# Block 0's MLP down in seven products at the end, the last mixer between its upward groups, second products accumulated on copies in PSUM

## The chip, the cores and the metric

The kernel runs on one core of a Trainium2 chip. The metric is the device time of one execution in microseconds (us); the median of three runs is 498.36 us (498.01 to 498.67). A core has five engines with their own in-order instruction streams: TensorE (PE, matmuls), VectorE (DVE), ScalarE (ACT), GpSimd (POOL) and SyncE (SP, which here only issues transfers). PSUM has eight banks into which matmuls write; SBUF holds everything else on chip.

## What is computed

The reference, cut to what matters; all numbers are float32, with 2048 rows (S), 512 columns (D), 32 heads of 16 and a hidden width of 1376 (F):

```
xn  = layernorm(x)
q, k, v = heads of xn @ wqkv
phi(t)  = where(t > 0, t + 1, exp(t)) + 1e-6
kv  = einsum("bhsd,bhse->bhde", phi(k), v);  z = sum over s of phi(k)
s   = (phi(q) @ kv) / (phi(q) . z + 1e-6), heads joined, @ wo
h   = gelu(layernorm(xn) @ w1)          # the mixer
hs  = h with its four column groups shifted by +1, -1, +2, -2 rows, @ w2
x1  = xn + hs
h2  = gelu(layernorm(x1) @ w3) @ w4     # the MLP: "up" by w3, "down" by w4
out = x + s * silu(x1 + h2)
```

## The kernel before

**Rows and precision.** The 2048 rows are four blocks of 512, each of four row tiles of 128 (QT = 4, NQ = 4). A float32 product is made of three matmuls: each operand is split into a rounded high part and the remainder (`rounded`: ScalarE copies the high part, VectorE subtracts it), and `products` issues high x high, high x low and low x high into one PSUM bank. TH = 256 is half a block.

**Seven products.** Most large products are cut in 2 x 2 and made of seven products of half size in place of eight; the sums and differences of the quarters are formed beforehand. The function `seven` runs one such group in three banks: pb, pe and pa. The first product, a11·b11, stands in pb and is copied to SBUF (p1) by ScalarE; a12·b21 goes to pa, and VectorE adds pa and p1 to the first result. The rest of pb and pe follows with more products accumulated on the same bank, each after a copy of what stood there. The mixer (`mix2`), the ways up (`up_pair`, `up_late`) and the attention (`attend_pair`) use it; the projections have their own version.

**The plan.** The kernel function does not issue instructions in the order in which it names them. Each call adds an operation to a list with an estimated duration. `Plan.emit` then walks the list with a model of the engines: TensorE's operations follow roughly their named order (within a window), the other engines' operations get due times worked back from it, and each may open its buffers only some microseconds ahead of its due time. The table SOONER shifts the due times of single operations, by their number in the list. Buffers come from pools with slots: 90 of 512 columns in SBUF ("p"), 6 of 256 ("h"), and in PSUM two pools of four banks, "mm" and "acc".

**The order of the work.** First the keys, queries and their gram matrices for all blocks; then the mixer of blocks 0 to 3 (`join_a`, `mix1`, `forms`, `mix2`), with the folding of kv and wo into one matrix M between them; then the MLP and the attention together. In the MLP the hidden width is eleven slices of 128, the last with 96: five pairs (s, s + 5), NS = 5, and a last one. `turn_y` prepares a block's normalised rows, `load_pair` the slices of w3, `up_last` and five ways up follow.

Block 0 differs from the others (LATE = 1, 2, 3). Its ways up (`up_pair`) put gelu's result out twice, as high part and as full value, and VectorE forms the remainder. Its way down (`down`) follows slice by slice between the ways up: for each slice and each of four row tiles three matmuls of 512 columns, accumulated over all eleven slices in the four banks of the "acc" pool (tiles acc0_0 to acc0_3). Its w4 slices are read through `load_w4` (six of them split early, `make_w4`, and stored in the memory array w4d; five made on the way).

Blocks 1 to 3 go up with `up_late`, which keeps gelu's results in SBUF, and are taken down at the end in the order LINE = (2, 3, 1): `down_forms` builds the sums of the quarters and their high and low parts, `down_late` makes the seven products, with banks from both PSUM pools. Block 1 (SPILL) is written to the array hd by `put` and read back at the end; its sums s1 and s3 are made by an accumulating transfer on POOL's queue (`gather`). Its attention result goes through the array sod in the same way.

The attention runs in pairs of row tiles at places given by ATT (`turn_q`, `forms_q`, `attend_pair`). `gate` multiplies by the attention result, adds x by a transfer and stores the output; for block 0 it uses tanh and two VectorE operations, for the late blocks silu and one.

Of the kernel before, what the change touches and what calls it, by code (L numbers as in the profile page):

```python
# [8 lines left out]
F32 = mybir.dt.float32  # L9
# [5 lines left out]
P = 128  # L15
# [9 lines left out]
class Tile:  # L25


    def __init__(self, plan, tag, name, dtype, width, rows=P):
        self.plan, self.tag, self.name, self.dtype, self.width, self.rows = plan, tag, name, dtype, width, rows
        self.ap = None  # L30
        self.log = []
        self.left = 0
        self.end = 0.0
        self.psum = tag in plan.psum
        self.early = plan.early

# [49 lines left out]
class Plan:  # L86
# [198 lines left out]
    def emit(self, first, lead, reserve, window, ahead, table=()):  # L285
# [16 lines left out]
        table = 0  # L302
        done = set()
        slip = 0.0
        left = len(ops)
        while left:
# [56 lines left out]
            for t in op.tiles:  # L363
                if t.ap is None:
                    tag = t.tag
                    if tag in slots:
                        t.slot = slots[tag].pop(0)[1]
                        tag += str(t.slot)
                    t.ap = self.pools[t.tag].tile([t.rows, t.width], t.dtype, tag=tag, name=t.name)
# [42 lines left out]
def linear_attn_gated_by_mixer(  # L412
# [62 lines left out]
    def bank(name):  # L475
        return pl.new("mm", name, F32, 512)[:, :]
# [154 lines left out]
    def spread(b):  # L631
# [7 lines left out]
        ps = pl.new("mm", f"ab{b}", F32, 512)[:2 * QT, :P]  # L639
# [289 lines left out]
    def seven(name, z, prod):  # L929

        pa, pb, pe = (bank(f"{n}{name}").cols(0, TH) for n in ("pa", "pb", "pe"))
        p1, p5, u2 = (pl.new("h", f"{n}{name}", F32, TH).all for n in ("p1", "p5", "u2"))

        def go(ps, x, y, start=True):
            products(ps, prod(x, y), start, more=not start)

# [212 lines left out]
    def make_w4(f):  # L1149
        n = rows(f)  # L1150
        st, (hi, lo) = piece(f"w4_{f}_s").rows(n), rounds(f"w4_{f}")
        pl.load(st, w4[f * P:f * P + n, :])
        rounded(hi.rows(n), lo.rows(n), st)
        for k, v in enumerate((hi, lo)):
            keep_in(w4d[f], k, v.rows(n), n)
        return hi.rows(n), lo.rows(n)

    def load_w4(b, f):
        n = rows(f)
        if b == 0 and f not in early_f:  # L1160
            W4[b, f] = make_w4(f)
            return
        W4[b, f] = tuple(v.rows(n) for v in rounds(f"w4_{b}_{f}"))
        for k, v in enumerate(W4[b, f]):
            pl.fetch(v.f32, w4d[f][:n, k * 512:(k + 1) * 512])
# [104 lines left out]
    def up_last(b):  # L1270
# [4 lines left out]
        late = b in LATE  # L1275
        if late:
            HL[b] = ge.rows(n)
        else:
            hi, lo = rounds(f"f{b}_{f}")
        for t in range(2):  # L1280
            h = t * TH, (t + 1) * TH
            ps = bank(f"a{b}_{f}_{t}").cols(0, TH).rows(n)
            ks = y[f"b1{t + 1}"] + y[f"b2{t + 1}"]
            products(ps, [AF3["last"][c] + ks[c] for c in range(NC)])
            if not late:
                pl.act(hi.cols(*h).rows(n), ps, AF.Gelu_apprx_tanh)
            pl.act(ge.cols(*h).rows(n), ps, AF.Gelu_apprx_tanh)
        if late:
            if b in SPILL:
                put(b, 10, HL[b], n)  # L1290
            return
        split(lo.rows(n), ge.rows(n), hi.rows(n))
        H3[b, f] = (hi, lo, n)

    def up_pair(b, s):
        hi, lo = zip(*(rounds(f"f{b}_{f}") for f in (s, s + NS)))
        full = [piece(f"gf{b}_{f}") for f in (s, s + NS)]
        c1, c2 = full
        z = c1.cols(0, TH), c1.cols(TH, 512), c2.cols(TH, 512)
        ps = seven(f"{b}_{s}", z, lambda x, y: [AF3[s][x][c] + YT[b][y][c] for c in range(2)])  # L1300
        pl.act(hi[0], c1, AF.Gelu_apprx_tanh)
        pl.act(c1, c1, AF.Gelu_apprx_tanh)
        split(lo[0], c1, hi[0])
        pl.act(hi[1].cols(TH, 512), z[2], AF.Gelu_apprx_tanh)
        pl.act(z[2], z[2], AF.Gelu_apprx_tanh)
        pl.act(hi[1].cols(0, TH), ps, AF.Gelu_apprx_tanh)
# [629 lines left out]
```

## Time and profile before

| | |
|---|---|
| median of three runs | 498.36 us |
| span of the profiled execution | 496.4 us |
| instructions in it | 9885 |
| TensorE busy | 490.6 us (99%) |
| VectorE busy | 438.4 us (88%) |
| ScalarE busy | 373.4 us (75%) |
| GpSimd busy | 123.6 us (25%) |
| transfers | 117.44 MB, 237 GB/s on average |

The time of the profiled execution outside its span is not recorded; the median of the runs is 1.96 us above that span. Names in the profile are those of the program's tiles with their numbers left out: acc are block 0's accumulators, pb, pe and pa the banks of the ways up, pbm of the mixer, pbs, pes and pas of the attention, pbd, ped and pad of the late ways down. Most operations are recorded in helpers, so their line is that of the helper (L146 for a matmul, L168 for ScalarE, L191 and L201 for VectorE, L225 for POOL's transfers); the tile tells them apart. A matmul's duration in the profile includes its way through the array, so the pitch is read from start to start.

### The profile page before, as it was taken

How to read it: one execution, taken by the hardware profiler on the slowest of the kernel's cores; microseconds unless marked ns; L12 is line 12 of the kernel's file. 1: busy time of each engine (PE TensorE's matmuls, PEld its weight loads, DVE VectorE, ACT ScalarE, POOL GpSimd, SP SyncE). 2: the span in 40 equal slices, each digit the busy share in tenths (PEclk: the TensorE clock that was granted, in tenths of full speed). 3: DMA queues.
4: the chain of work that ended last, by engine and by line, in shares of the span. 5: the costliest groups of instructions: out<-in, count | busy, mean ns of one | idle time of the engine just before them, and what ended most of it. 6: DMA issues, size and time to landing. Idle time of an engine off the chain costs nothing.

```text
span 496.4 us, 9885 instructions
## 1 busy us (share of the span) xinstructions
PE 490.6 (99%) x3244; PEld 447.0 (90%) x3244; DVE 438.4 (88%) x874; ACT 373.4 (75%) x845; POOL 123.6 (25%) x214
## 2 busy tenths in 40 slices
PE   8999999999999999999999999999999999999996
PEld 6778888888888999899889999999999999999996
DVE  5998997889989669999999999999999899796864
ACT  5999999677887599999988567765686877565531
POOL 1384404276930232133200021100000000143420
PEclk9999999999999999999999999999999999999999
DMA  7869696999974999999988499984634699599996
GB/s 229 303 187 297 133 296 183 237 287 269 329 220 100 236 310 248 273 252 290 337 268 247 158 194 298 247 262 138 183 114 147 215 336 332 114 226 283 278 224 182
DMA packets 87082, 117.44 MB, mean 237 GB/s; under 512 B 10328, under 2 KB 39160, under 8 KB 87032
## 3 DMA queue, kind: packets, MB, share of 16 engines
q1 hardware_dynamic: 75512, 96.11, 59.6%
q0 software_dynamic: 11520, 20.71, 24.9%
q8 instruction: 25, 0.41, 0.4%
q14 instruction: 25, 0.20, 0.1%
HBM read 72.66 MB, written 39.93 MB: 227 GB/s over the span
## 4 chain that ended last, share of the span: by engine, by line
PE 97%; DMA 1%; SPq 1%; ACT 0%; DVE 0%; issue 0%; ACTq 0%
PE pb L146 12%; PE pbd L146 9%; PE h L146 9%; PE g L146 9%; PE acc L146 6%; PE pe L146 6%; PE pbx L146 6%; PE ped L146 5%; PE pbm L146 5%; PE pbs L146 5%; PE q L146 3%; PE pa L146 3%; PE pex L146 3%; PE k L146 3%; PE pad L146 3%; PE pes L146 2%
## 5 line engine op out<-in xcount | busy, mean ns | idle before, releaser
L225 POOL DMA_DIRECT2D xo<-x1d x12 | 10.9, 950 | 166.2 <-DVE xo L191 118.5
L225 POOL DMA_DIRECT2D th<-in_x x14 | 12.2, 895 | 45.0 <-DVE th L201 23.1
L225 POOL DMA_DIRECT2D o<-xnd x16 | 14.0, 887 | 37.5 <-DVE o L191 13.5
L168 ACT ACTIVATE th<-xo 128x512 f32<-128x512 f32 (+1 forms) x16 | 9.7, 614 | 15.9 <-DVE xo L201 10.1
L225 POOL DMA_DIRECT2D zacc<-ke x12 | 12.9, 1073 | 31.4 <-DMA zacc<-ke 10.4
L191 DVE TENSOR_TENSOR ht<-h,abc 128x512 f32<-128x512 f32 x16 | 11.0, 690 | 7.5 <-PE h L146 7.4
L225 POOL DMA_DIRECT2D xt<-nrow x16 | 14.6, 1288 | 8.4 <-ACT k12h L168 4.1
L196 POOL TENSOR_SCALAR w<-mv 128x4 f32<-128x4 f32 (+2 forms) x10 | 2.5, 254 | 40.7 <-ACT sq L168 40.4
L168 ACT ACTIVATE y<-o,nm,rs 128x512 f32<-128x512 f32 x16 | 12.4, 814 | 0.2 <-POOL nm L196 0.2
L168 ACT ACTIVATE p<-pb 128x256 f32<-128x256 f32 x20 | 7.6, 381 | 5.8 <-PE pb L146 5.4
L168 ACT ACTIVATE ht<-ht 128x512 f32<-128x512 f32 x16 | 10.0, 626 | 2.1 <-DVE ht L191 2.0
L168 ACT ACTIVATE sq<-o,mv 128x512 f32<-128x512 f32 x16 | 11.5, 722 | 0.1
L168 ACT ACTIVATE u<-pb 128x256 f32<-128x256 f32 x20 | 7.7, 383 | 5.1 <-PE pb L146 4.5
L201 DVE SCALAR_TENSOR_TENSOR pq<-pq,rd 128x512 f32<-128x512 f32 x16 | 11.0, 688 | 0.3
L168 ACT ACTIVATE p<-pe 128x256 f32<-128x256 f32 x20 | 7.7, 384 | 4.6 <-PE pe L146 4.1
L201 DVE SCALAR_TENSOR_TENSOR qz<-pq,zb 128x512 f32<-128x512 f32 x16 | 10.8, 682 | 0.0
L1471 DVE TENSOR_REDUCE den<-qz 128x32 f32<-128x512 f32 x16 | 10.8, 679 | 0.0
L168 ACT ACTIVATE sq<-o 128x512 f32<-128x512 f32 x16 | 10.0, 629 | 0.1
L613 POOL TENSOR_TENSOR rs<-w,nhalf 128x4 f32<-128x4 f32 (+2 forms) x10 | 9.7, 970 | 0.8
L168 ACT ACTIVATE x<-x,nm,rs 128x512 f32<-128x512 f32 x12 | 9.2, 805 | 0.0
L201 DVE SCALAR_TENSOR_TENSOR th<-th,so 128x512 f32<-128x512 f32 x12 | 8.2, 683 | 0.6 <-ACT th L168 0.5
L168 ACT ACTIVATE sq<-x,mv 128x512 f32<-128x512 f32 x12 | 8.6, 718 | 0.1
(2075 smaller groups left out, 2446.9 us busy)
## 6 DMA issues: line engine op xcount, KB each, us to landing
w_s<-in_w SPq DMA_DIRECT2D x28, 256.0 KB, 5.6
x<-in_x SPq DMA_DIRECT2D x16, 256.0 KB, 6.2
xt<-in_xt SPq DMA_DIRECT2D x16, 256.0 KB, 6.9
xnd<-x SPq DMA_DIRECT2D x16, 256.0 KB, 5.9
xt<-nrow POOLq DMA_DIRECT2D x16, 256.0 KB, 7.6
pqd<-qr SPq DMA_DIRECT2D x16, 256.0 KB, 6.1
o<-xnd POOLq DMA_DIRECT2D x16, 256.0 KB, 6.6
x1d<-o SPq DMA_DIRECT2D x16, 256.0 KB, 5.1
```

Of the source, the lines that this page charges most:

```text
L146: lambda: nc.tensor.matmul(out.get(), lhs.get(), rhs.get(), start=start, stop=stop, skip_group_check=more))
L168: nc.scalar.activation(out.get(), src.get(), func, scale=get(scale), **kw)
L191: self.vec(eng, out, [a, b], lambda: self.e(eng).tensor_tensor(out.get(), a.get(), b.get(), op=op), True)
L196: lambda: self.e(eng).tensor_scalar(out.get(), a.get(), get(s1), get(s2), **kw), False,
L201: lambda: self.nc.vector.scalar_tensor_tensor(out.get(), a.get(), get(s), b.get(), op0=op0, op1=op1),
L225: lambda: self.nc.gpsimd.dma_start(out.get(), get(src), accum_op=ALU.add), mb=mb)
L613: lambda: g.tensor_tensor(out.get(), src.get(), nh.get(), op=ALU.pow))
L1471: pl.add("DVE", .6, .68, [t], [den], lambda: nc.vector.tensor_reduce(den.get(), t.get().rearrange("p (h d) -> p h d", d=DH), axis=AX.X, op ...
```

## The change

1. Block 0 is treated like the other blocks. It goes up with `up_late`, is written to hd, and is taken down at the end in the seven-product form, third of four (LINE = 2, 3, 0, 1). `up_pair`, `down`, `load_w4` and the accumulators are gone, and its gate is the silu form.
2. The w4 slices are now split only for the stored copy. Five are split early, five at places given by W4_AT, and of the slices 0 to 4 only the left half is split and stored. The split of the folded matrix's quarter b12, which nothing reads, is gone.
3. The last block's mixer (`join_a`, `mix1`, `forms`, `mix2` of block 3) moves in between block 0's ways up, by `lastly`. `forms_m` moves to the start of block 1, and the attention pairs start at (1, 1) and end at (3, 4).
4. In `seven`, for ways up and attention (not the mixer), ScalarE copies the first product to a bank of the other pool, and the second product is accumulated there. Gelu or the attention's copy reads that bank directly, so VectorE's first add is gone. The two pools change places from one group to the next. The order of the products changes: a11·b11, s1·t1, then a12·b21. The planner also keeps account of which banks a product has written.
5. The table SOONER has new entries throughout (left out below).

```diff
-    EARLY = (), (10, 0, 5, 1, 6, 2)
-    LATE = 1, 2, 3
-    SPILL = 1,
-    LINE = 2, 3, 1
+    EARLY = (), (0, 5, 1, 6, 2)
+    LATE = 0, 1, 2, 3
+    SPILL = 0, 1
+    LINE = 2, 3, 0, 1
-    ATT = {(0, 5): (0,), (1, 1): (2,), (1, 3): (4,), (2, 0): (6,), (2, 2): (8,), (2, 4): (10,), (3, 1): (12,), (3, 3): (14,)}
+    ATT = {(1, 1): (0,), (1, 3): (2,), (2, 0): (4,), (2, 2): (6,), (2, 4): (8,), (3, 0): (10,), (3, 2): (12,), (3, 4): (14,)}
+    W4_AT = {(0, 4): 7, (1, 0): 3, (1, 2): 8, (1, 4): 4, (2, 1): 9}
...
+    TURN = ["mm", "acc"]
+
+    def seven(name, z, prod, first=None):
+
+        here, there = "mm", "acc"
+        if first is not None:
+            here, there = TURN[:] = TURN[::-1]
+        pb, pe = (bank(f"{n}{name}", here).cols(0, TH) for n in ("pb", "pe"))
+        p5, u2 = (pl.new("h", f"{n}{name}", F32, TH).all for n in ("p5", "u2"))
...
+        if first is not None:
+            pa = bank(f"pa{name}", there, "onto").cols(0, TH)
+            go(pb, "a11", "b11")
+            pl.act(pa, pb, AF.Copy)
+            go(pe, "s1", "t1")
+            pl.act(p5, pe, AF.Copy)
+            go(pa, "a12", "b21", False)
+            first(pa)
+            go(pb, "s2", "t2", False)
+            pl.act(u2, pb, AF.Copy)
+            go(pe, "s4", "b22", False)
+            pl.tt(z[1], u2, pe, ALU.add)
+            go(pb, "s3", "t3", False)
+            pl.tt(z[2], pb, p5, ALU.add)
+            go(pb, "a22", "t4", False)
+            return pb
...
     def make_w4(f):
-        n = rows(f)
-        st, (hi, lo) = piece(f"w4_{f}_s").rows(n), rounds(f"w4_{f}")
-        pl.load(st, w4[f * P:f * P + n, :])
-        rounded(hi.rows(n), lo.rows(n), st)
+        n = TH if f < NS else 512
+        st, (hi, lo) = piece(f"w4_{f}_s").cols(0, n), both(rounds(f"w4_{f}"), 0, n)
+        pl.load(st, w4[f * P:(f + 1) * P, :n])
+        rounded(hi, lo, st)
...
     def up_late(b, s):
...
-        ps = seven(f"{b}_{s}", (a11, a21, a22), lambda x, y: [AF3[s][x][c] + YT[b][y][c] for c in range(2)])
-        for v in (a11, a21, a22):
+        ps = seven(f"{b}_{s}", (a11, a21, a22), lambda x, y: [AF3[s][x][c] + YT[b][y][c] for c in range(2)],
+                   lambda pa: pl.act(a11, pa, AF.Gelu_apprx_tanh))
+        for v in (a21, a22):
             pl.act(v, v, AF.Gelu_apprx_tanh)
...
     def attend_pair(i):
...
-                   lambda x, y: [QF[i][x][c] + M[y][c] for c in range(2)])
+                   lambda x, y: [QF[i][x][c] + M[y][c] for c in range(2)],
+                   lambda pa: pl.act(o1.cols(0, TH), pa, AF.Copy))
...
-    b = 3
-    join_a(b)
-    for gg in ORDER:
-        mix1(b, gg)
...
-    forms(b)
-    mix2(b * QT)
-    mix2(b * QT + 1)
...
-    forms_m()
+    def lastly(s):
+        b = NQ - 1
+        if s == 1:
+            join_a(b)
+            for gg in ORDER:
+                mix1(b, gg)
+        elif s == 2:
+            forms(b)
+        elif s > 2:
+            mix2(b * QT + s - 3)
+
     for b in range(NQ):
-        if b in LATE:
...
-        A = [pl.new("acc", f"acc{b}_{j}", F32, 512) for j in range(QT)]
...
-            if n > 0 and n - 1 < len(groups) - 2:
-                for f in groups[n - 1]:
-                    for j in range(QT):
-                        down(b, f, j, A[j])
...
+        if b == 1:
+            forms_m()
+        up_last(b)
+        for s in range(NS):
+            if b == 0 and s < NS - 1:
+                load_pair(s + 1)
+            if s == NS - 1 and b < NQ - 1:
+                turn_y(b + 1)
+            if b == 0:
+                lastly(s)
+            up_late(b, s)
+            attends((b, s))
+            if (b, s) in W4_AT:
+                make_w4(W4_AT[b, s])
+            for k in SUMS.get((b, s), ()):
+                sums_w4(k)
```

More of the change, by code (lines that the diff above doesn't have):

```diff
@@ L368, in emit @@
                         tag += str(t.slot)
+                        if t.sums is not None:
+                            if t.sums == "onto" and tag not in written:
+                                raise RuntimeError(f"{t.name}: bank {tag} not written by a product")
+                            (written.discard if t.sums == "part" else written.add)(tag)
                     t.ap = self.pools[t.tag].tile([t.rows, t.width], t.dtype, tag=tag, name=t.name)
@@ L1573, in gate @@
         pl.store(out[i * P:(i + 1) * P, o:o + w], th)
-    warm = bank("warm")
+    warm = bank("warm", sums="part")
     for n in range(WARM):
@@ L1583, in linear_attn_gated_by_mixer @@
     wneg = piece("wneg")
-    G = [pl.new("acc", f"g{c}", F32, 512) for c in range(NC)]
+    G = [bank(f"g{c}", "acc").tile for c in range(NC)]
     def load_rows(i):
@@ L1602, in linear_attn_gated_by_mixer @@
     ks[1:] = [bank(f"k{i}") for i in range(1, QT)]
[L1603 removed]
+    ksum = bank("ksum", "acc")
     for i in range(2):
```

119 lines of the change are left out of this document (18 added, 101 removed), and 129 rows, old and new, of the table SOONER.

## The prediction

> **What bounds the kernel now.** I read the page's head and slices first, then the waits of TensorE, then busy time by stretch, then the chain of work that ended last.
>
> ```profile
> span 496.4 us, 9885 instructions
> PE 490.6 (99%) x3244; PEld 447.0 (90%) x3244; DVE 438.4 (88%) x874; ACT 373.4 (75%) x845; POOL 123.6 (25%) x214
> ...
> PE   8999999999999999999999999999999999999996
> ...
> DVE  5998997889989669999999999999999899796864
> ...
> PE 97%; DMA 1%; SPq 1%; ACT 0%; DVE 0%; issue 0%; ACTq 0%
> ```
> ```profile
> PE warm L146 <- POOL ones L529: 1.1, 1, 1.1
> PE k L146 <- DVE u_1l L191: 0.4, 1, 0.4
> ```
> ```profile
> 130.00:185.00 55.00, 55.00 (x305) 47.55 (x305) 44.41 (x92) 41.85 (x91) 17.28 (x38) 1.00 0.81 225
> 185.00:404.00 219.00, 218.93 (x1662) 209.80 (x1661) 212.15 (x440) 173.71 (x434) 25.02 (x34) 1.00 0.82 231
> 290.00:404.00 114.00, 113.93 (x956) 113.40 (x955) 109.69 (x231) 79.69 (x205) 5.19 (x6) 1.00 0.74 207
> 404.00:496.40 92.40, 88.07 (x745) 87.86 (x743) 70.43 (x141) 46.44 (x100) 21.06 (x24) 0.99 0.91 243
> ```
>
> The waits name TensorE twice, both in the first microseconds, 1.5 us together; from 185 to 404 it is busy for 218.93 of 219 us, at a granted clock of 1.00, and 97% of the chain is TensorE. So time is the number of matmuls times their pitch. A busy TensorE may still run late inside a busy stretch, so I take the pitch from pieces of the chain with one tile alone (start, us, number of matmuls): "acc" streams 512 columns, "pbd" 256. The two pieces of "pb" between them show what the chain mostly looks like: after nine to twelve matmuls it changes to another tile.
>
> ```profile
> 244.46 3.46 PE acc L146 x15
> ...
> 283.14 3.72 PE acc L146 x16
> ...
> 345.23 1.40 PE pb L146 x12
> ...
> 378.37 1.10 PE pb L146 x9
> ...
> 427.89 10.79 PE pbd L146 x91
> ...
> 458.45 7.80 PE pbd L146 x66
> ```
>
> 3.46/15 and 3.72/16 are 230.7 and 232.5 ns; 10.79/91 and 7.80/66 are 118.6 and 118.2 ns. I use 231.6 and 118.4. Against that, 290 to 404 holds 956 matmuls, nearly all of 256 columns: 956 x 0.1184 = 113.2 of 114 us, so under 1 us of hidden lateness there. VectorE is second: 212.15 of 219 us busy between 185 and 404, its slices mostly at 9. It is the engine that could become the bound.
>
> **The change part by part.**
>
> *Block 0's way down.* Before, 11 slices of the hidden width x 4 row tiles x 3 products of 512 columns. The trace has all of them (matmuls are the PE column):
>
> ```profile
> 212.00:300.00 88.00, 35.93 (x132) 22.84 (x132) 2.40 (x4) 1.00 0.89 248
> ```
>
> 132 x 0.2316 = 30.57 us. After, block 0 goes through the seven-product form like the other blocks: per pair of row tiles 7 products x 5 slices x 3 matmuls, and 4 x 3 for the last slice, 117; two pairs, 234 matmuls of 256 columns: 234 x 0.1184 = 27.71 us. Gain 2.86 us (2.70 to 3.03 with the extreme pitches). Everything else on TensorE keeps its count: the ways up were seven products already, the mixer and the attention are only moved. It is gain on the path, as TensorE never rests.
>
> The Trainium skill, "TensorE: Matmul & The Clock Gate", section "Back-to-back issue gap", states a sustained spacing of about 81 ns for 128 columns and 131 ns for 512. Interpolated that is an estimate of 98 ns for 256, and 132 x 131 against 234 x 98 ns would cost 5.6 us instead. The chain's 118 and 232 ns disagree with it.
>
> *VectorE.* Four things leave the stretch 185 to 404. Rows are groups with count, us, mean ns:
>
> ```profile
> L191 DVE TENSOR_TENSOR h_a110f<-pa,p 128x256 f32<-128x256 f32 x6 | 2.5, 421 | 0.1
> L191 DVE TENSOR_TENSOR h_a111f<-pa,p 128x256 f32<-128x256 f32 x6 | 2.5, 421 | 0.0
> L191 DVE TENSOR_TENSOR h_a11xf<-pa,p 128x256 f32<-128x256 f32 x3 | 1.3, 420 | 0.0
> L191 DVE TENSOR_TENSOR gf<-pa,p 128x256 f32<-128x256 f32 x5 | 2.0, 410 | 0.2 <-PE pa L146 0.2
> L191 DVE TENSOR_TENSOR f_5l<-gf,f_5h 128x512 fp32r<-128x512 f32 x1 | 0.7, 694 | 0.0
> L191 DVE TENSOR_TENSOR so<-so,xo 128x512 f32<-128x512 f32 x4 | 2.7, 683 | 0.0
> L201 DVE SCALAR_TENSOR_TENSOR th<-th,so 128x512 f32<-128x512 f32 x12 | 8.2, 683 | 0.6 <-ACT th L168 0.5
> ```
> ```profile
> L191 DVE TENSOR_TENSOR so<-pas,p1s x8: 410/420/425, 281.7 to 400.3; 128x256 f32<-128x256 f32 x8
> ```
>
> The first add of 28 sevens (20 up, 8 attention) goes, because the second product is now accumulated on the copy: 2.5 + 2.5 + 1.3 + 2.0 + 8 x 0.42 = 11.7 us. Block 0's eleven remainders go: 11 x 0.69 = 7.6. Its gate leaves for the end: 2.7 + 4 x 0.687 = 5.4. One unused split of the folded projection, one split of the last w4 slice and halves of others are dropped: about 1.7. Sum 26.4 us of durations. VectorE's durations overlap (440 instructions add up to some 243 us in 212 busy, my sum over that stretch), so I count 0.87 of it, 23.0 us. What stays is 189.2 us, in a stretch that is now 219 - 30.6 = 188.4 us of TensorE. So VectorE has no room at all there unless about 1 us or more is done earlier or later. Room exists: 10.6 us of idleness from 130 to 185 (44.41 of 55), where w3 pairs may be made ahead, and 22 us after 404. I cost it at nothing while that cover holds; without it each us is a us.
>
> *Copies in PSUM.* The copy of the first product goes to another bank instead of SBUF, and TensorE's second product must now wait for it. Durations:
>
> ```profile
> 299.75 0.41 ACT L168 ACTIVATE h_a210f<-h_a210f 128x256 f32<-128x256 f32 x1
> ...
> 301.04 0.62 ACT L168 ACTIVATE q2s0h<-q2f 128x512 fp32r<-128x512 f32 x1
> ...
> 302.69 0.28 PE L146 MATMUL pbs<-m_b11h,q2l 128*128 128x256 f32 x1
> ...
> 303.00 0.38 ACT L168 ACTIVATE p1s<-pbs 128x256 f32<-128x256 f32 x1 [0.47 <-PE pbs L146]
> ...
> 303.92 0.36 ACT L168 ACTIVATE h_a120f<-pb 128x256 f32<-128x256 f32 x1
> ```
>
> The copy ends 0.69 us after the last product's start (302.69 to 303.38). Six products s1·t1 stand between, 6 x 0.118 = 0.71 us: just enough if ScalarE is free. If it has just begun a 0.62 us split, up to 0.6 us is missing, 28 x 0.6 = 17 us at worst; 0 at best, and not below, since nothing starts earlier for it. No row has ScalarE writing PSUM; 0.38 is the nearest. The same spacing exists already: the u2 copy reads the bank that s3·t3 writes six products later, in all 28, and TensorE's waits list none. I take 0.01 us each, 0.3 in all. Behind a waiting product stands every later matmul. The gelu that read SBUF after the add (0.41) now reads PSUM (0.36): ScalarE about even, +8 copies of 0.38 for the attention, less block 0's doubled gelus. At 173.71 of 219 us it has room. Both pools now give banks to sevens in turn, eight instead of four once block 0's accumulators are gone; a gain of 0 to the 0.8 us of lateness above; I take 0.
>
> *Last mixer between block 0's groups.* Same instructions, later: one row fetch, 48 + 84 matmuls, 4 gathers and a power step on POOL, 4 stores of x1 and 4 of the turned y on SP. Their reader is block 3's way up, some 80 us on; POOL was busy 25.02 of 219 us. Block 0's own ways up come earlier by those 21 us (48 x 0.2316 + 84 x 0.1184), so what feeds them must too: that is the pairs above. Attention starts two groups later, forms_m with it, the five late w4 slices later still; all are wanted only in later blocks. Cost nothing, covered by the same VectorE room.
>
> *Spill and fetch.* Block 0's hidden tile goes to memory and returns.
>
> ```profile
> L219 SPq DMA_DIRECT2D d1f_s10f<-hd x1: 320/320/320, 433.8 to 433.8; - x1
> L225 POOL DMA_DIRECT2D d1f_s10f<-hd x1: 1555/1555/1555, 438.6 to 438.6; - x1
> ...
> DMA to landing us min/median/max: 4.1/7.8/11.4
> ```
> ```profile
> L219 SPq DMA_DIRECT2D h_ba110f<-hd x1: 422/422/422, 445.9 to 445.9; - x1
> L168 ACT ACTIVATE d_a110h<-h_ba110f x1: 623/623/623, 453.5 to 453.5; 128x512 fp32r<-128x512 f32 x1
> ```
> ```profile
> DMA packets 87082, 117.44 MB, mean 237 GB/s; under 512 B 10328, under 2 KB 39160, under 8 KB 87032
> ```
>
> Added: 11 + 4 stores, 16 + 4 fetches, 6 accumulating gathers, 9.7 MB. Dropped: 12 fetches of w4 in block 0, and half of many w4 loads and stores, 5.6 MB. The net 4.1 MB is 3.5% of 117.44 MB. The end stretch gets more: some 5.8 MB of fetches, and 3.1 MB that move there (x1 and x gathers, out). 243 GB/s x 92.4 us + 8.9 MB over 120 us is 261 GB/s, against 243 before, at a busy share of 0.91 that would become 0.98. Cover: block 1's forms were issued from 433.8 on, its first one, a11, at 445.9 and read at 453.5, 7.6 us later, where a landing takes 4.1 to 11.4. That is thin, but TensorE did not stop for it. I cost it at 0; if the cover is gone, one form that lands at 11.4 instead of 7.8 is some 3.6 us late, of which the earlier block's last products hide perhaps half: 2 us. The block's VectorE work at the end, 21 remainders, 6 sums, 6 results, 4 gates, about 19 us, fits its 27.7 us of TensorE.
>
> **Sum.** 496.4 - 2.86 + 0.3 = 493.8 us of span. The median of the runs, 498.36, is 1.96 above this profile's span; with the same around it, 495.8 us.
>
> **The rivals.**
>
> (a) *VectorE becomes the bound* between the last mixer and the first way down. 189.2 us of work against 188.4 is the argument for; against, 10.6 us idle just before. If nothing moves out and it keeps half of its former idleness (half of 219 - 212.15 = 3.4), the stretch lasts 192.6, 4.2 us more: 500.0 us. It decides from 191.3 us on, where the 2.9 are eaten. This is the one that ends slower.
>
> (b) *The copies hold TensorE.* ScalarE is busy 79% of the time; half of a 0.62 us operation ahead, 0.79 x 0.31 = 0.24 us, times 28, is 6.9 us bare. The chain's other pieces are mostly five to twelve matmuls of changing tiles, so other groups fill such gaps; with three quarters filled 1.7 stay: 497.2. TensorE's empty list of waits speaks against it.
>
> (c) *Late transfers at the end.* One late form of block 0 or block 1, 2 us: 497.5. For: the share of 0.98 and the thin cover. Against: block 1 lived with the same, and the in-order queue can issue block 0's fetches during all of block 3's way down.
>
> (d) *The hidden lateness goes too*, with eight banks and fewer adds: 0.8 us between 290 and 404 and as much again ahead of it: 494.2.
>
> (e) *A matmul costs by the instruction, not by the column.* The change adds 102 instructions. The gain is gone at 132 x 0.2316 / 234 = 131 ns for 256 columns, which gives 498.4; every 10 ns beyond cost 2.3 us. The rows leave a fixed part of 2 x 118.4 - 231.6 = 5 ns in each, not the 30 this needs. The section of the Trainium skill named above would put the time on this side.
>
> **How the numbers follow.** Forecast 0.51 (own range 494.9 to 496.7), (a) 0.19, (b) 0.11, (c) 0.08, (d) 0.10, (e) 0.01. A measurement can tell about 0.2%, 1.0 us. Faster, below 497.4: forecast, (d) and a little of (b), 0.64. Slower, above 499.4: most of (a), 0.17. Same: the rest, 0.19. The range leaves out the worse half of (a) and the better half of (d): 494.2 to 499.2.
>
> **What would show it.** Right: no tile acc with 512-column matmuls after the keys; 234 more of 256 columns named pad, pbd, ped; a PE list of waits still empty after the start; span near 493.8; no add of pa and p on VectorE. Wrong by (a): slices of PE below 9 before the first way down, with VectorE at 9; by (b): PE waits on ScalarE at pa or pas; by (c): PE waits in the last 120 us behind fetches; by (e): pbd pieces over 125 ns a matmul.

## The result, and the profile after

| | kernel before | changed kernel |
|---|---|---|
| median of 4 runs | 498.51 us (498.01 to 499.01) | 501.78 us (501.69 to 503.58) |
| ratio | | 1.0072, interval 1.006 to 1.0085 |
| span of the profiled execution | 496.4 us | 500.1 us |

The changed kernel is 3.3 us slower. 495.8 us was forecast, with 499.2 as the upper end. Ratios, here and below, leave out an execution that is more than 1.5% above the fastest of its kernel; of the kernels below that is one, the 506.65 us of after_wide_order.

From the page of the changed kernel: its head, the slices of TensorE and VectorE, the packets, and the shares of the chain of work that ended last, by engine:

```profile
span 500.1 us, 10206 instructions
...
PE 490.2 (98%) x3346; PEld 448.8 (90%) x3346; DVE 433.9 (87%) x863; ACT 378.8 (76%) x865; POOL 130.8 (26%) x220
...
PE   8999999999999999999999999999999999999996
...
DVE  5898788897999869999999999899999977878754
...
DMA packets 90925, 121.60 MB, mean 243 GB/s; under 512 B 10744, under 2 KB 42392, under 8 KB 90872
...
PE 73%; DMA 11%; DVE 5%; ACT 4%; POOL 3%; issue 2%; SPq 1%; DVEq 0%; POOLq 0%; ACTq 0%
```

The matmuls are the 3,244 + 102 of the forecast, and the bytes are 4.2 MB more, where 4.1 were forecast. What is new is the chain: TensorE was 97% of it before and is 73% now, and 11% are transfers. The six longest pieces of the chain that are transfers, and one piece of TensorE (start, us, what):

```profile
36.12 9.89 DMA xt<-nrow
...
58.11 10.61 DMA xt<-nrow
...
195.18 7.31 DMA o<-xnd
...
316.40 5.33 DMA q9d<-q9z
...
401.88 9.11 PE pbd L147 x77
...
432.59 7.22 DMA xo<-x1d
...
444.65 8.62 DMA xo<-x1d
```

The line of pbd is a piece of TensorE with one tile alone: 9.11/77 = 118.3 ns for 256 columns, so the pitch hasn't changed. With the pitch one can part what TensorE does from what it is late by. I cut the trace at the first matmul into g, pax (the keys in sevens), h (the mixers), a (the ways up) and pbd (the late ways down), and at the last matmul. Between two marks I count the matmuls by width, take 231.6 ns for 512 columns and 118.3 for 256 (428 and 215 for the few in full fp32; the few others, of 128 columns, are priced alike in both kernels), and call what the stage took beyond that its lateness. A value of -0.19 shows how exact such prices are:

| stage | work before | work after | late before | late after | difference |
|---|---|---|---|---|---|
| start to first g | 15.29 | 15.29 | 2.66 | 3.16 | +0.50 |
| to keys in sevens | 34.46 | 34.93 | 0.59 | 0.64 | +0.05 |
| to the mixers | 74.87 | 75.10 | 0.17 | 1.36 | +1.19 |
| to the ways up | 95.83 | 76.21 | -0.19 | 0.69 | +0.88 |
| to the ways down | 178.56 | 166.80 | 0.93 | 2.75 | +1.82 |
| to the last matmul | 87.54 | 115.34 | 0.02 | 2.21 | +2.19 |
| sum | 486.55 | 483.67 | 4.18 | 10.81 | +6.63 |

The work fell by 2.88 us, and the lateness rose by 6.63: together +3.75 us, which is the span's +3.7. Two fifths of it (+2.6 us) arise before the ways up, where the change adds no matmul and no copy from bank to bank.

The first five of TensorE's nine waits in the changed kernel (what it waited with, for what; us, times, longest):

```profile
PE ped L147 <- ACT d_s40h L169: 1.2, 1, 1.2
PE pa L147 <- ACT pa L169: 1.1, 1, 1.1
PE warm L147 <- POOL ones L539: 1.0, 1, 1.0
PE k L147 <- ACT u_2h L169: 0.4, 1, 0.4
PE qsum L147 <- DVE wqt L192: 0.4, 1, 0.4
```

The list was to stay empty after the start. The two longest lines name ScalarE, and read alone they would speak for rival (b), the copies. The rows of ScalarE's queue ahead of them say otherwise (start, us; in brackets the idle time before and what ended it):

```profile
319.28 0.62 ACT L169 ACTIVATE q6s0h<-q6f 128x512 fp32r<-128x512 f32 x1
321.81 0.63 ACT L169 ACTIVATE q6s1h<-q6f 128x512 fp32r<-128x512 f32 x1 [1.91 <-DMA q9d<-q9z]
322.35 0.40 ACT L169 ACTIVATE h_a221f<-h_a221f 128x256 f32<-128x256 f32 x1
322.66 0.36 ACT L169 ACTIVATE pa<-pb 128x256 f32<-128x256 f32 x1
...
450.54 0.40 ACT L169 ACTIVATE d_a11xh<-h_ba11xf 128x256 fp32r<-128x256 f32 x1
453.36 0.63 ACT L169 ACTIVATE th<-xo 128x512 f32<-128x512 f32 x1 [2.42 <-DMA xo<-x1d]
453.90 0.37 ACT L169 ACTIVATE p5d<-ped 128x256 f32<-128x256 f32 x1
454.16 0.62 ACT L169 ACTIVATE d_s40h<-d0f_s40f 128x512 fp32r<-128x512 f32 x1
```

At 319.9 ScalarE reaches a rounding whose buffer a store was still reading, and stands for 1.91 us; behind it stands the copy pa<-pb. At 450.9 it is a gate whose xo a gather is still adding to, 2.42 us; the rounding d_s40h, which stands behind it, is the one TensorE waits for: its product started 1.47 us after the product before. The names in TensorE's list are the last links of such rows, not the first.

### The profile page after: what moved, and what is told of

Same layout as the page of the kernel before. It is cut to its first block, busy times and chain, and to the rows that moved or that the text cites. A ratio compares the mean times of both kernels' runs of the same rounds, so it can differ in the third digit from the quotient of the medians.

```text
span 500.1 us, 10206 instructions
## 1 busy us (share of the span) xinstructions
PE 490.2 (98%) x3346; PEld 448.8 (90%) x3346; DVE 433.9 (87%) x863; ACT 378.8 (76%) x865; POOL 130.8 (26%) x220
## 4 chain that ended last, share of the span: by engine, by line
PE 73%; DMA 11%; DVE 5%; ACT 4%; POOL 3%; issue 2%; SPq 1%; DVEq 0%; POOLq 0%; ACTq 0%
PE pb L147 11%; PE pbd L147 10%; PE h L147 8%; PE ped L147 6%; PE g L147 6%; PE pe L147 6%; PE pbs L147 4%; PE pbx L147 4%; DMA xt<-nrow 4%; DMA xo<-x1d 3%; PE pa L147 3%; PE pad L147 3%; PE pbm L147 2%; PE a L147 2%; PE pes L147 2%
## 5 line engine op out<-in xcount | busy, mean ns | idle before, releaser
L226 POOL DMA_DIRECT2D zacc<-ke x12 | 11.3, 939 | 29.9 <-DMA zacc<-ke 14.5
L202 DVE SCALAR_TENSOR_TENSOR xo<-pbd,p5d 128x256 f32<-128x256 f32 x8 | 3.4, 423 | 9.5 <-PE pbd L147 9.5
L623 POOL TENSOR_TENSOR rs<-w,nhalf 128x4 f32<-128x4 f32 (+2 forms) x10 | 11.4, 1138 | 0.7
L1461 DVE TENSOR_REDUCE den<-qz 128x32 f32<-128x512 f32 x16 | 10.8, 677 | 0.3
L202 DVE SCALAR_TENSOR_TENSOR pq<-pq,rd 128x512 f32<-128x512 f32 x16 | 10.8, 676 | 0.1
L202 DVE SCALAR_TENSOR_TENSOR qr<-qe,qi 128x512 f32<-128x512 f32 x11 | 7.5, 686 | 2.1 <-ACT qe L169 2.1
L169 ACT ACTIVATE pa<-pb 128x256 f32<-128x256 f32 x20 | 7.4, 372 | 1.5 <-PE pb L147 1.4
```

Of the source, the lines that this page charges most:

```text
L169: nc.scalar.activation(out.get(), src.get(), func, scale=get(scale), **kw)
L202: lambda: self.nc.vector.scalar_tensor_tensor(out.get(), a.get(), get(s), b.get(), op0=op0, op1=op1),
L226: lambda: self.nc.gpsimd.dma_start(out.get(), get(src), accum_op=ALU.add), mb=mb)
L623: lambda: g.tensor_tensor(out.get(), src.get(), nh.get(), op=ALU.pow))
L1461: pl.add("DVE", .6, .68, [t], [den], lambda: nc.vector.tensor_reduce(den.get(), t.get().rearrange("p (h d) -> p h d", d=DH), axis=AX.X, op ...
```

## The experiments

All but the kernels named otherwise start from the changed kernel with its order written out, so that an edit doesn't make the planner put everything in another order:

```diff
-    pl.emit(first=6.0, lead={"p": 9.0, "w": 20.0, "ab": 10.0}, reserve={"p": 8, "w": 1, "ab": 0}, window=9.0,
-            ahead=6.0, table=SOONER)
+    pl.in_order(ORDERED, SLOTS)
```

ORDERED is the list of instructions, SLOTS the buffer of each tile; instructions named in a third list are left out. Times are medians in us, the ratio is to the kernel before on the same chip (498.2 to 498.6).

**same_order**: nothing but this rewriting.

> Control. The changed kernel with the order of its instructions and the buffer of each tile written out as a list, in place of the planner that finds them; every engine gets the same instructions in the same order as before this rewriting. Every theory: the time of the changed kernel, ratio to the kernel before 1.006 to 1.0085, about 501.8 us. The three kernels beside it are changed from this list, without any planning anew.

502.34, ratio 1.0079 (1.0065 to 1.0093), span 500.6, lateness by stage 3.71, 1.12, 1.67, 0.92, 1.28, 2.66: 11.4 us. This is what the next five are held against. The stage from the ways up to the ways down is 2.75 us late in the changed kernel's profile and 1.28 in this one, with the same instructions in the same order on every engine; the wait at pa isn't in this list. So a single profile places about 1.5 us no better than that.

**no_copies**: rival (b).

```diff
-            go(pa, "a12", "b21", False)
+            go(pa, "a12", "b21")
...
+    WITHOUT = {2088, 2210, 2307,
...
+    pl.in_order(ORDERED, SLOTS, WITHOUT)
```

> The changed kernel in its own order without the 28 copies from bank to bank; the second product of each seven starts its bank anew, so the first product is missing from one of the four results. 28 x 0.372 us of ScalarE and 28 waits of TensorE for a copy go. Theory C (the copies hold TensorE, rival b of the prediction): 1.7 to 6.9 us less, 495 to 500. Theory Q: the copies themselves wait for nothing late, so only what ScalarE's queue saves by 10.4 us less work: 0 to 1 us, 500.8 to 501.9.

503.21, ratio 1.0091 (1.0075 to 1.0107): nothing gained. Lateness 12.7 us, with 3.53 between the ways up and down. So the copies do not hold TensorE by the 1.7 us of rival (b); what they cost is less than these runs can tell. In the changed kernel they took 372 ns (to PSUM) where the nearest row had been 0.38 us (to SBUF).

```profile
L169 ACT ACTIVATE pa<-pb 128x256 f32<-128x256 f32 x20 | 7.4, 372 | 1.5 <-PE pb L147 1.4
```

**less_vector**: rival (a).

```diff
+    WITHOUT = {2792, 2804, 2990,
...
```

> The changed kernel in its own order without the 16 in-place multiplications pq<-pq,rd on VectorE between 242 and 358 us (the attention is then not divided by its sums): 16 x 0.678 = 10.8 us less of VectorE's 182 in that stretch. Theory V (VectorE is the bound there, rival a of the prediction): what TensorE is late from the mixer to the way down, 2.2 to 3.4 us, goes: 499 to 500.3. Theory Q (single instructions blocked behind transfers): 0 to 1 us, 501.2 to 502.3.

501.86, ratio 1.0057 (1.0037 to 1.0078), which overlaps that of same_order. The stretch from 185 to 373.5 us in same_order and here (columns: PE, PEld, DVE, ACT, POOL busy, clock, DMA share, GB/s; the share adds up the times of all packets that start in the stretch, so it can pass 1):

```profile
185.00:373.50 188.50, 187.88 (x1519) 184.18 (x1518) 183.46 (x385) 159.54 (x414) 17.99 (x24) 1.00 0.80 237
```
```profile
185.00:373.50 188.50, 187.34 (x1515) 183.46 (x1515) 173.89 (x368) 157.98 (x411) 18.54 (x24) 1.00 0.80 235
```

VectorE has 9.6 us more room (173.89 busy, not 183.46), and TensorE does 1,515 matmuls in the stretch, not 1,519. The two stages there are late by 3.0 us (2.2 in same_order). VectorE's load is not what makes TensorE late, though it has little room: 5.0 us of 188.5 in same_order, where rival (a) had counted none.

**no_x_rows**: rival (c), less to move at the end.

```diff
+    WITHOUT = {4564, 4588, 4650, 4674, 4888, 4912, 4974, 4998, 5232, 5256, 5318, 5342, 5514, 5556}
```

> The changed kernel in its own order without the 14 gathers that add rows of x onto results between 409 and 490 us (so 14 row tiles of the output lack x): 3.7 MB less of what the last 96 us move, and 14 issues less in POOL's queue. Theory D (the transfers of the end are too many, so that all of them land late): the 2.2 us by which the way down runs late mostly go, 499.5 to 500.3. Theory Q: the waits that cost are those of single instructions in bad places, and most transfers they wait for are issued from other queues or before these: 0 to 1 us, 500.8 to 501.9.

500.54, ratio 1.0038 (1.0025 to 1.0051), 1.8 us less. The last stage is late by 0.13 us, not 2.66; the others keep theirs. From 427 to 475 us, same_order first, then this kernel:

```profile
427.00:475.00 48.00, 47.31 (x397) 46.97 (x396) 39.08 (x77) 27.04 (x58) 19.07 (x23) 1.00 1.09 275
```
```profile
427.00:475.00 48.00, 48.00 (x407) 48.00 (x406) 39.25 (x77) 26.56 (x57) 13.06 (x15) 1.00 1.00 252
```

The DMA engines' share falls from 1.09 to 1.00, and TensorE does ten matmuls more in the same 48 us. So the lateness at the end goes with the gathers of x. That transfers crowd each other there fits it, but this run doesn't part the 3.7 MB from the 14 issues on POOL, or from the buffers that come free earlier without them.

**two_buffers** and **one_gate**: take away the pauses at 321.7 and 453.4 us.

```diff
-        5420, 5171, 5044, 5172, 4996, 5173, 5174, 5175, 5176, 5396, 5039, 5202, 5203, 5177, 5204, 5205, 5206, 5126, 5207, 5040,
+        5420, 5171, 5044, 5172, 5173, 5174, 5175, 5176, 5396, 5039, 5202, 5203, 5177, 5204, 5205, 5206, 5126, 5207, 5040, 4996,
```

4996 is the gate th<-xo, 5040 the rounding d_s40h. In SLOTS two_buffers puts q6s1h into buffer 52 and d_s40h into 41; one_gate leaves q6s1h and puts d_s40h into 37. The tiles that come later in these buffers change places with them. In same_order the first of the two waits is absent and the second is 0.7 us long, not 1.2, so less is to be had than the changed kernel's own profile promised.

> The changed kernel in its own order, with two tiles in other buffers and one instruction of ScalarE moved: q6s1h goes to a buffer that no store is still reading, d_s40h to one that isn't block 3's xo, and the gate th<-xo of the last row tile of block 3 stands behind d_s40h in place of two ahead of it. Theory Q (an instruction that waits for a transfer stands in an in-order queue ahead of what TensorE wants next): the two gaps of TensorE at 321.7 and 453.4 us, 1.36 and 1.47 us, go, and the time falls by 1.5 to 2.8 us, to 499.0 to 500.3. Theory V (VectorE is the bound, and TensorE's lateness only comes out at these places): the lateness comes out somewhere else, 501.3 to 501.9.

506.76, ratio 1.0174 (1.0159 to 1.0189): 4.4 us slower, which no theory had. ScalarE, TensorE and the stretches around the place:

```profile
451.63 0.38 ACT L169 ACTIVATE p5d<-ped 128x256 f32<-128x256 f32 x1 [0.81 <-PE ped L147]
455.57 0.63 ACT L169 ACTIVATE d_s40h<-d0f_s40f 128x512 fp32r<-128x512 f32 x1 [3.56 <-DMA out<-th]
```
```profile
453.22 0.28 PE L147 MATMUL pbd<-wu_40h,d_s1xl 128*128 128x256 f32 x1
456.25 0.80 PE L147 MATMUL ped<-wf_b220h,d_s40h 128*128 128x256 f32 x2 [2.76 <-ACT d_s40h L169]
```
```profile
453.00:457.00 4.00, 1.24 (x8) 1.00 (x6) 0.25 (x1) 1.43 (x4) 0.00 (x0) 0.89 1.08 305
457.00:463.00 6.00, 5.84 (x27) 5.50 (x26) 4.47 (x10) 2.75 (x7) 1.75 (x2) 0.51 0.93 207
463.00:475.00 12.00, 12.00 (x104) 12.00 (x103) 8.79 (x18) 4.37 (x8) 3.48 (x4) 1.00 0.88 212
```

Buffer 41 had held th of an earlier row tile, and the store of that result was late as well: one late transfer was exchanged for a later one. And the pause had an echo. For the 6 us after it the granted clock was 0.51, and 27 matmuls took as long as some 51 take at 118 ns. Of the last stage's lateness of 7.56 us the pause is 2.9 (3.03 between the starts, less one pitch) and the slow clock 2.8 (6.0 less 27 x 0.118).

> The changed kernel in its own order, with the gate th<-xo of block 3's last row tile behind d_s40h in ScalarE's queue, and d_s40h in the buffer that d0f_s20f left (freed by VectorE at 452.2, no store to wait for). Theory Q (in-order queue blocked by a late transfer): TensorE's pause before ped at 453 to 455 us goes, 0.7 to 1.5 us less than the same kernel in its own order (502.3): 500.8 to 501.7. Theory V: 502.0 to 502.6.

501.73, ratio 1.0065 (1.0052 to 1.0078), 0.6 us less than same_order with overlapping intervals. The wait for d_s40h is out of TensorE's list; one of 0.7 us for its remainder d_s40l, on VectorE, has come in its place. The last stage is late by 1.51 us, not 2.66, while the stage before it is at 2.51, not 1.28, within what two executions of one order showed. So the rounding was late because of the gate ahead of it. What that is worth in time isn't settled by this run: 501.73 lies 0.03 us above the range of theory Q.

**after_new_order** and **before_new_order**: is the rest in the order?

> The changed kernel with every instruction and every buffer kept, and only the order within each engine's queue changed: instructions were moved past their neighbours, and a move was kept when it made the end earlier as a mean over many drawings of the transfers' landing times, with the scatter that the traces show (5.4 us in the mean, about 1.4 us up or down). Theory O (the change saves its 2.9 us of matmul, and the 6.6 us of lateness beside it belong to the order the instructions were put in, not to what the change does): most of the 6.6 us go, 495 to 498 us, faster than the kernel before. Theory S (lateness comes with the change itself: more transfers at the end, copies, VectorE without room): no order removes it, 500 to 503.

> The kernel before, its order searched in the same way and for as long. Theory O: it is hardly late anywhere (TensorE's lateness in it is 4.2 us, 2.7 of them in the first 20 us), so little is to be had: 496.5 to 499.5; the difference to the changed kernel in its new order is then the change alone, some 2 to 3 us. Theory S: the same time here, and the changed kernel stays above it.

509.26 (504.04 to 510.46), ratio 1.0217 (1.0191 to 1.0242), and 504.00, ratio 1.0109 (1.0095 to 1.0122): both theories missed, both kernels got slower. What the first of them has to tell is in its stages: up to the mixers it is late by 2.38, 0.16 and 0.92 us, 3.46 together, where same_order has 6.50 and the kernel before 3.42. Between the ways up and down it is late by 5.38. This profile is of an execution of 504.04 us; the four others took 507.14 to 510.46, so what made them longer is not in it.

**front_order**: its front alone.

> The changed kernel in its own order, but for the instructions that its order has in the first 160 us: these (keys, queries, k sums and the first two mixers, which the change does not touch) take the order that the run after_new_order had. There TensorE was late by 2.38, 0.16 and 0.92 us in the three stages up to the mixer, against 3.71, 1.12 and 1.67 us in the changed kernel's own order (3.3 before). Theory O (the lateness belongs to the order): the front gives back about 3 us, and the rest, unchanged, keeps its own lateness: 498.5 to 500. Theory V (VectorE bounds the way from the mixer to the first way down, so time saved ahead of it is lost in it): 501.5 to 502.5.

508.21, ratio 1.0193 (1.0164 to 1.0221). Theory O missed by 8 us, and V's range as well. The stage from the first g to the keys in sevens, 0.16 us late in after_new_order with the same order, is late by 8.47 here. The longest wait, POOL's rows that made it, and VectorE's last instruction before it paused:

```profile
PE ab L152 <- POOL an L197: 5.2, 1, 5.2
```
```profile
32.08 4.08 POOL L197 TENSOR_SCALAR an<-mv 128x4 f32<-128x4 f32 x1
...
36.51 1.04 POOL L646 TENSOR_TENSOR an<-pu,nhalf 128x4 f32<-128x4 f32 x1
...
51.36 0.23 POOL L197 TENSOR_SCALAR an<-mv 128x4 f32<-128x4 f32 x1
```
```profile
35.37 0.69 DVE L192 TENSOR_TENSOR kq_f<-wk_s,wq_s 128x512 f32<-128x512 f32 x1
```

The same instruction on 128x4 elements takes 4.08 us once and 0.23 us another time. The long one ends at 36.16, 0.10 us after a row of VectorE's instructions without a pause; VectorE's next starts at 38.06. The product ab, for which TensorE paused, stood behind it. In the starts of the matmuls this pause is 5.3 us long, and the matmuls after it are 2.8 us slow, at a granted clock of 0.50: 8.1 of the 8.47 us. So this run doesn't test what the front's order is worth; it shows that the same order can be 0.16 or 8.47 us late in this stage. Whether the longer executions of after_new_order paused at this place is not known.

**after_wide_order** and **before_wide_order**.

> The changed kernel's instructions and buffers in a third order, searched from its own one with two things drawn at random for each trial: the landing of every transfer (scatter 1.2 us), and the pitch of VectorE's and ScalarE's instructions, 0 to 12 and 4 to 17 ns longer than the planner takes them, since in the trace of the changed kernel they are about 10 and 15 ns longer. Theory O with room for both uncertainties: 494.5 to 498, below the kernel before. If it is above 500, an order made by a model of these queues cannot win the matmuls back, or the change itself makes TensorE late (theory S).

> The kernel before with its order searched in the same way. Theory O: 496 to 499, at least 1.5 us above the changed kernel so ordered. Theory S: below or level with the changed kernel so ordered.

502.33, ratio 1.0055 (1.0023 to 1.0087), and 500.38, ratio 1.0036 (1.0022 to 1.005): both above the ranges of theory O, and the changed kernel above the other, as theory S had it. The changed kernel's 11 runs go from 498.28 to 506.65. Its profiled execution is late by only 3.2 us up to the ways up (7.4 in same_order, 3.2 before) and by 4.94 after them, 3.1 of it in one pause of TensorE at 212 to 215 us. Behind it, POOL, then VectorE, then ScalarE:

```profile
207.61 4.75 POOL L734 TENSOR_TENSOR u_2l<-hal,u_2h 128x2 fp32r<-128x2 f32 x1
212.44 0.19 POOL L197 TENSOR_SCALAR w<-mv 128x4 f32<-128x4 f32 x1
212.72 1.05 POOL L646 TENSOR_TENSOR rs<-w,nhalf 128x4 f32<-128x4 f32 x1
...
214.13 0.23 POOL L197 TENSOR_SCALAR nm<-nm 128x4 f32<-128x4 f32 x1
```
```profile
207.66 0.68 DVE L192 TENSOR_TENSOR yb210l<-y_0t,yb210h 128x512 fp32r<-128x512 f32 x1
...
211.61 0.68 DVE L192 TENSOR_TENSOR w_s1l<-w_sf,w_s1h 128x512 fp32r<-128x512 f32 x1
215.24 0.71 DVE L156 STREAM_TRANSPOSE y_0z<-y 128x512 f32<-128x512 f32 x1 [2.94 <-ACT y L169]
```
```profile
214.39 0.81 ACT L169 ACTIVATE y<-o,nm,rs 128x512 f32<-128x512 f32 x1 [3.34 <-POOL nm L197]
215.11 0.36 ACT L169 ACTIVATE u<-pb 128x256 f32<-128x256 f32 x1
```

From 207.66 on VectorE goes from one instruction with two operands in SBUF to the next, until 212.29. POOL's subtraction of 128x2 elements begins at 207.61 and ends at 212.36, just behind it. The power step for a row of the mixer stands behind the subtraction, ScalarE's y<-o,nm,rs behind the power step, and behind that the copy u<-pb, for which TensorE paused. It is an in-order queue once more, only that what is late is a small instruction and no transfer.

**after_pool_order**, **after_pool_order2** and **before_pool_order**: orders that allow for it.

> The changed kernel's instructions and buffers in an order that was searched with three things drawn at random: where transfers land, the pitch of VectorE and ScalarE, and how long POOL's small instructions take. The last is new: in after_wide_order u_2l<-hal,u_2h, 128x2 elements, took between 186 and 4746 ns, the long one from 207.61 to 212.35 us, while VectorE went from one instruction to the next until 212.30; behind it stood the power step for a row of the mixer, so ScalarE's y<-o,nm,rs waited, and behind that the copy u<-pb for which TensorE paused 3.24 us. Theory P (the spread of 498.28 to 506.65 us among the runs of that order was made by POOL's small instructions that are held up for as long as VectorE doesn't pause): the spread shrinks to about 2 us and the median falls to 495.5 to 498.5, below the kernel before. Theory S (the change itself makes TensorE late): still above 500.

> The same search, begun from the changed kernel's own order and with other drawings; a second sample of what such an order gives. Theory P: 495.5 to 498.5 again, with a spread of about 2 us. Theory S: above 500.

> The kernel before, order searched in that way. Theory P: 497.5 to 500, and 1 to 3 us above the changed kernel in such an order, which is then what the change itself saves. Theory S: level with it or below.

| | median (range) | ratio (interval) | lateness |
|---|---|---|---|
| after_pool_order | 498.91 (497.9 to 500.85) | 1.0015 (1.0003 to 1.0028) | 6.6 |
| after_pool_order2 | 501.62 (500.85 to 503.96) | 1.0067 (1.0047 to 1.0087) | 10.6 |
| before_pool_order | 501.57 (501.05 to 502.52) | 1.0065 (1.0053 to 1.0077) | 7.6 |

The first order brings the changed kernel from 502.34 to 498.91 us with the same instructions and buffers, far outside the intervals (ratio 1.0079 to 1.0015); the spread is 3 us, not the 8 of after_wide_order. 498.91 lies 0.4 us above the range of theory P and below that of S. The second order and before_pool_order lie above P's ranges. The lateness of the first order by stage is 3.88, 0.16, 0.21, 0.29, 1.31, 0.79. From 427 to 475 us:

```profile
427.00:475.00 48.00, 48.00 (x406) 48.00 (x405) 37.83 (x74) 24.33 (x54) 16.78 (x19) 1.00 1.05 256
```

TensorE is full there although the kernel still makes all its transfers, so the lateness at the end isn't bound to their number. But in these 48 us it moves hardly more than no_x_rows (256 and 252 GB/s, same_order 275): the order also spreads the transfers, and the row doesn't part a smaller crowd from instructions that bear it better. So 4.7 us of the lateness of same_order belonged to the order, most of it between the first g and the mixers (2.4 us) and at the end (1.9); 3.4 us of it reach the time, and about 1 us is lost again behind the last instructions (the end came 3.99 us after VectorE's last one, 2.95 in same_order). The second order is no better than the changed kernel's own, so such an order is luck as well as care. Against before_pool_order the changed kernel is 2.7 us faster in the first order and level in the second.

**pool_order_head** and **pool_order_ends**: the rest, place by place.

> The order of after_pool_order, with the first 18 us in the order of after_new_order. TensorE was late by 3.88 us in its first stage in the former (x<-in_x goes out ahead of weights that the first products wait for) and by 2.38 and 2.20 us in the two runs that had the latter. Theory O (what TensorE is late by is set by the order in which it stands, place by place): 1.4 us less than after_pool_order (498.9): 497 to 498, at or below the kernel before. Rival F (an order is a whole: what is saved at one place changes the landing of all that follows and is lost again): 498.5 to 501.

> The same, and the last 20 us in the changed kernel's own order, whose end came 2.9 us after VectorE's last instruction where after_pool_order took 4.0 us. Theory O: another 0 to 1 us less: 496 to 498. Rival F: 498.5 to 501.

499.82, ratio 1.0022 (1.0009 to 1.0036), and 499.92, ratio 1.0016 (1.0 to 1.0031): both in the range of rival F. The first product of the kind g came hardly earlier (3.62 and 3.28 us late, not 3.88), though these first instructions alone had been 2.2 and 2.4 late with another order behind them, and nothing of it reached the end. With the old tail the end came 2.92 us after VectorE's last instruction, as it should, but the last stage was late by 2.32 us, not 0.70. No version that was run beats the kernel before; the best, 498.91 us, is 0.15% above it.

## Why the prediction was wrong, by its own steps

- **Fewer matmuls, 2.86 us.** Right: 2.88 us by count and pitch, 118.3 ns for 256 columns (118.4 assumed). Rival (e) is out.
- **The sum.** Here is the step that failed: "496.4 - 2.86 + 0.3" carries the lateness of the kernel before over unchanged, and prices only the waits that the edits name. But the planner's table of due times was exchanged with them, and so each queue got another order from the first microseconds on, also in the front, where both kernels plan the same instructions. The prediction had the table in front of it and gave it no term; the new order, with what the edits add to it, measured +6.63 us of lateness. after_pool_order shows that an order of the same instructions can be 4.7 us less late, and with it nearly all of the 3.3 us by which the changed kernel was slower is gone. How the 6.63 us part between the order and the edits is not shown.
- **"Copies in PSUM", 0.3 us, rival (b) 1.7.** The 0.3 is neither shown nor refuted: without the copies nothing was gained. The sign named for (b), TensorE's waits on ScalarE at pa, did appear (1.1 us), and came from a store that ScalarE waited for two instructions earlier. It was no sign of (b).
- **VectorE, rival (a), 500.0.** The time came out on that side, 1.8 us above it, but not by this way: that is luck. Forecast were 189.2 us of work in 188.4; same_order has 183.46 in 188.5, and 10.8 us less work of VectorE left the lateness of its stretch where it was.
- **"Spill and fetch", cost 0; rival (c), 2 us.** The load was forecast well: 261 GB/s at a share of 0.98 over 120 us, and the trace has 262 at 1.01. Wrong was the cost of 0: the last stage was late by 2.21 us, and by 0.13 without the gathers of x. The size is that of rival (c), the transfer is not. (c) spoke of a late form of block 0 or 1, and from 400 us on such a fetch held ScalarE once, for 0.6 us. The longest pause of TensorE, 1.35 of the 2.21 us, came from a gather of x1 for block 3's gate. The form d0f_s40f behind it was ready at 452.2 us and was rounded only at 454.2. So the cover of the forms held, and the gathers, which the prediction counted as bytes alone, were the ones that came late. The 0.98 was a mean, too: the share is 1.09 from 427 to 475 us in same_order. (By its own terms (c) gives 495.8 + 2 = 497.8 us, not 497.5.)

```profile
378.00:498.00 120.00, 116.53 (x978) 115.79 (x976) 91.76 (x180) 63.36 (x136) 33.15 (x38) 1.00 1.01 262
```
```profile
ACT d_a22xh L169 <- DMA h_ba21xf<-hd: 0.6, 1, 0.6
```

- **Moved mixer, cost 0.** No run parts it from the rest. The stage that it left rose by 0.88 us of lateness and the one it went to by 1.82; with after_pool_order they are late by 0.29 and 1.31 (before: -0.19 and 0.93).
- **Rival (d)**, that the hidden lateness goes: the opposite happened.

What stays open: how much of the lateness in the front and the middle each difference in the order makes, what the edits themselves add to it, and what the change is worth when its order is as good as that which the kernel before has. The search found no order for the kernel before that comes near its own (500.4, 501.6, 504.0 against 498.4), so it says little on how good one for the changed kernel could be. The 2.88 us of work are shown; that they can be had as time is not.

## What to carry to other kernels

Where every engine is full and runs its queue in order, a change is priced in two parts: the work that it takes from the bounding engine, and the lateness of the new order. Anything that makes a scheduler place the work anew puts the second part up for grabs, and here it was worth more than twice the first; hold the order fixed to measure an edit, and judge orders by how they bear late transfers and held instructions, not by their end on paper. When TensorE's list of waits names an engine, go up that engine's queue to the first row with idle time in brackets: the cause stands there.

## What the runs showed of the hardware that was not expected

A pause of TensorE can cost twice. After the 2.76 us of idle time in two_buffers the granted clock was 0.51 for 6 us, after the 5.2 us in front_order 0.50 (first row), and after the pause at 212 to 215 us in after_wide_order it was lower for some 4 us (PEclk is third from the right):

```profile
36.20:42.00 5.80, 5.79 (x15) 4.54 (x16) 1.44 (x2) 5.38 (x12) 4.75 (x7) 0.50 0.58 115
```
```profile
215.00:217.00 2.00, 1.47 (x7) 1.48 (x8) 1.23 (x2) 2.00 (x5) 0.53 (x1) 0.55 0.45 32
217.00:219.00 2.00, 2.00 (x8) 1.59 (x7) 1.95 (x6) 1.74 (x5) 0.00 (x0) 0.60 1.01 272
```

The pauses of 1.2 and 1.1 us in the changed kernel left it at 1.00. The Trainium skill, "TensorE: Matmul & The Clock Gate", section "What's actually happening", says that the clock falls to half after an idle window of about 3.4 us. The traces agree on the half; here 2.76 us of idle time were enough.

POOL's smallest instructions can take 25 times as long as they need. All eight u_2l<-hal,u_2h of after_wide_order (least, median and most ns):

```profile
L734 POOL TENSOR_TENSOR u_2l<-hal,u_2h x8: 186/645/4746, 128.7 to 207.6; 128x2 fp32r<-128x2 f32 x8
```

The long one lasted for as long as VectorE did not pause, as that of 4.08 us in front_order did; those of 3.94 us in before_pool_order (at 237.01) and 4.42 us in pool_order_ends (at 49.80) end 0.05 us after VectorE's last instruction before a pause as well (in the row of the former stands a reciprocal with one operand, which did not let POOL in). So it isn't the change that makes them. In before_wide_order one of 5.13 us (at 36.02) ends while VectorE is busy: 0.04 us after its last instruction with two operands in SBUF, when it has gone on to qi<-q,rs,cq, which reads q from PSUM. These are matches in time, and spans on POOL are rough; no run took VectorE's instructions away to test them. The Trainium skill, "GPSIMD Engine Reference", section "Key points", says that the two share SBUF interfaces and contend when VectorE's instruction has two SBUF inputs. The rows above agree; that it can hold an instruction of two elements a partition for eight of VectorE's in a row is what this case adds.
